# A time-mixing and MoE kernel on one core: unit 0 in two halves, three weight tiles in plain fp32, ten tiles of block 1 in halves, a new order table

## The chip, the cores and the metric

The kernel runs on one core of a Trainium2 chip. It uses TensorE (PE in the profile, with its weight loads as PEld), VectorE (DVE), ScalarE (ACT), GpSimd (POOL), SyncE (SP, which issues nearly all loads and stores), and the 16 DMA engines. The metric is the device time of one execution, in microseconds (us). Before the change it was 486.84 us, the median of three.

## The reference

Two stages, all in fp32. The first is a recurrence over 768 positions for 4 batches and 8 heads of 48 channels; the second is a two-layer network over the 3072 tokens that it gives.

```python
for t in range(S):                                    # S = 768
    cur = np.einsum('bhd,bhe->bhde', u[None] * kt, vt)
    y[:, :, t] = np.einsum('bhd,bhde->bhe', rt, state + cur)
    state = wt[:, :, :, None] * state + np.einsum('bhd,bhe->bhde', kt, vt)
...
h = x @ w_in                                          # (3072, 384) @ (384, 2048)
g = np.where(h >= 1, h, np.where(h <= -1, 0, (h + 1) ** 2 / 4))
out = g @ w_out                                       # (3072, 2048) @ (2048, 384)
```

## The kernel before, in words

**First stage.** The 768 positions are cut into 12 units of 64 positions (256 tokens over the four batches). `attention(u)` does one unit. Its heads come in two groups q = 1 and q = 0. For each group DVE scans the decays w from the end (`scan`, L451) and from the start (L456) and scales k and r by them (`scaled`, L474); ACT forms u times k (`with_u`, L479). PE multiplies r with u times k (the diagonal) and scaled r with scaled k, in 32 products of 64 x 64 each (`among`, L508). DVE picks the diagonal of the first result and the upper part of the second into R by masked copies (`picked`, L516). PE transposes k (L558), forms the state (`umat`, L583), and multiplies R and the old state with v and r (`along` and `crossed`, L618). Units 0 and 1 have one head per group spread over three places; PE brings it there (`spread`, L709). ACT then writes x rounded to fp32r (x high, L688), PE subtracts it in PSUM (`less`, L699), and ACT writes the rest (x low, L684).

**Second stage.** Six blocks of 512 tokens, two units each; 16 weight tiles of 128 columns of the hidden layer (ff tiles). A product of fp32 accuracy is made of three fp32r products (high x high, high x low, low x high), so nine matmuls of one tile into the hidden layer (`product_in`, L1262) and nine out of it (`product_out`, L1282). Between them ACT and DVE apply the gate (L1062, L1063, L1072) and split g into high (ACT, L1074) and low (DVE, L1075). Weight tiles are loaded as raw bits, put together into the fp32 tile `fl` by two ACT passes and two DVE passes (L347, L352, L366, L369), and split into high (L343 on ACT, for two tiles L341 on DVE) and low (L373). There are three `fl` buffers. Where a unit's x is there before the block's second unit, tiles are done for 256 tokens at a time ("in halves"): block 0 for tiles 0 to 4, block 1 for tiles 0 to 13. Blocks 3 to 5 use a scheme with fewer products (L932).

**Order.** Every step is entered into a list by `op`; the table `ORDER` gives the order in which the steps are emitted to the engines' queues, `BANKS` which of the eight PSUM banks each result gets, and `FILLS` where products of zeros (`zeros`, L298) are put in on PE. Each engine works through its queue in that order and waits where its operands or its bank aren't ready. So the names ps, rk, xf, x, fl in the profile are tiles; rk holds r and k, wq the decays, cst the constants.

Of the kernel before, what the change touches and what calls it, by code (L numbers as in the profile page):

```python
# [25 lines left out]
C = 64  # L26
# [10 lines left out]
PAIRED = [(i, i + 1) for i in range(0, 14, 2)]  # L37
# [95 lines left out]
)  # L133
FILLS = (
    (42, 0, 256, False), (50, 0, 512, False), (54, 0, 384, False),
)

LOW = 7.499 * 2.0**-32


class Plan:
# [26 lines left out]
    def emits(self, fill):  # L168

        put_in = {n: x for n, *x in FILLS}  # L170
        for n in ORDER:
            if n in put_in:
                fill(*put_in[n])
            self.ops[n]["emit"]()
# [1171 lines left out]
```

## Time and profile before

| | us |
|---|---|
| three timed executions | 486.79, 486.84, 489.51 |
| median | 486.84 |
| the profiled execution, first to last instruction | 489.6 |
| PE, DVE, ACT, POOL busy in it | 470.8, 403.1, 301.8, 28.1 |

No other time is given for the profiled execution than its span. PE busy is the time in which at least one matmul is in the array; matmuls overlap, so the time from one row's start to the next row's start tells more than the sum of durations. A timeline row merges instructions of one form; its second number reaches from the first start to the last end. The clock column gives the granted clock as a share of 2.4 GHz.

### The profile page before, as it was taken

Reading aid. Unit: us, or ns where it says so; the run is one execution under the profiler, and the core shown is the slowest. Engines: PE = TensorE matmul, PEld = TensorE weight load, DVE = VectorE, ACT = ScalarE, POOL = GpSimd, SP = SyncE. Lnnn points to the kernel's source line nnn. Section 1 sums busy time; section 2 is a strip of 40 time slices with the busy share of each in tenths; the row PEclk is TensorE's granted clock in tenths of the full one; section 3 lists DMA queues with packets and bytes.
Section 4 is the critical chain, followed back from the end, with each engine's and each line's share of the span. In section 5 each row is a group of like instructions: output and inputs, shape, how many; then the busy total and the mean of one; then the engine's idle time right before and its main releaser. Section 6 shows DMA issues by size and latency. Waiting matters only on the chain.

```text
span 489.6 us, 13368 instructions
## 1 busy us (share of the span) xinstructions
PE 470.8 (96%) x5709; PEld 417.4 (85%) x5709; DVE 403.1 (82%) x627; ACT 301.8 (62%) x582; POOL 28.1 (6%) x49
## 2 busy tenths in 40 slices
PE   2899999999999999999999999999999999999994
PEld 2689888889999999888888888999889999889984
DVE  6899999999897888798998977889687657585682
ACT  4788988854635276365655567855846656776560
POOL 4000000000000000000000033412300000000000
PEclk9999999999999999999999999999999999999998
DMA  8939646324650435243444201110010111121102
GB/s 317 384 134 325 263 174 205 105 70 147 199 169 3 148 111 170 100 168 105 149 154 138 85 3 50 46 23 15 9 39 28 45 23 21 33 76 44 23 1 72
DMA packets 35205, 53.53 MB, mean 109 GB/s; under 512 B 15744, under 2 KB 22592, under 8 KB 35136
## 3 DMA queue, kind: packets, MB, share of 16 engines
q1 hardware_dynamic: 34992, 52.45, 32.3%
q8 instruction: 47, 0.77, 0.7%
q14 instruction: 22, 0.18, 0.1%
q10 hardware_dynamic: 144, 0.13, 0.1%
HBM read 46.86 MB, written 4.72 MB: 105 GB/s over the span
## 4 chain that ended last, share of the span: by engine, by line
PE 85%; DVE 5%; DMA 5%; issue 2%; SPq 2%; ACT 1%; DVEq 0%
PE ps L1262 37%; PE ps L932 19%; PE ps L1282 18%; PE ps L618 4%; PE ps L508 3%; PE ps L558 2%; DMA rk<-in_rk 2%; DMA wq<-in_w 2%; PE ps L583 2%; DMA nk<-in_nk 1%; DVE y L451 1%; SPq L730 1%; SPq L280 1%; DVE fl L369 1%; DVE rk L474 0%
## 5 line engine op out<-in xcount | busy, mean ns | idle before, releaser
L1262 PE MATMUL ps<-x,wt 128*128 128x512 f32 (+1 forms) x1035 | 214.0, 357 | 0.1
L1262 PEld LDWEIGHTS ps<-x,wt 128*128 128x128 f32 x1035 | 168.1, 188 | 26.8 <-DVE rk L894 0.4
L1282 PE MATMUL ps<-gh,wt 128*128 128x256 f32 (+1 forms) x402 | 79.3, 332 | 0.4 <-DVE g L1072 0.4
L1282 PEld LDWEIGHTS ps<-gh,wt 128*128 128x128 f32 x402 | 61.5, 188 | 7.9 <-DVE g L1072 0.6
L892 ACT ACTIVATE rk<-ps 128x512 f32<-128x512 f32 x48 | 28.4, 597 | 46.3 <-PE ps L1262 27.3
L894 DVE SCALAR_TENSOR_TENSOR rk<-rk,ps 128x512 f32<-128x512 f32 x48 | 32.6, 684 | 24.1 <-ACT rk L893 23.9
L1062 ACT ACTIVATE g<-ps 128x512 f32<-128x512 f32 (+1 forms) x49 | 28.7, 588 | 34.7 <-PE ps L1262 23.1
L1282 PE MATMUL ps<-gl,wt 128*128 128x256 f32 (+1 forms) x201 | 44.1, 328 | 0.0
L1074 ACT CAST gh<-g 128x512 fp32r<-128x512 f32 (+1 forms) x49 | 29.5, 609 | 18.4 <-DVE g L1072 18.4
L1072 DVE SCALAR_TENSOR_TENSOR g<-g,ps 128x512 f32<-128x512 f32 (+1 forms) x49 | 32.2, 665 | 6.3 <-ACT g L1063 6.3
L1075 DVE TENSOR_TENSOR gl<-g,gh 128x512 fp32r<-128x512 f32 (+1 forms) x49 | 32.9, 678 | 4.1 <-ACT gh L1074 3.9
L1282 PEld LDWEIGHTS ps<-gl,wt 128*128 128x128 f32 x201 | 32.3, 188 | 3.6
L451 DVE TENSOR_TENSOR_SCAN y<-wq,ends 128x520 f32<-128x520 f32 x24 | 29.6, 1234 | 5.5 <-POOL r L289 3.8
L900 DVE TENSOR_TENSOR g_again<-rk,nk_again 128x512 fp32r<-128x512 f32 x35 | 24.5, 711 | 11.3 <-ACT nk_again L899 11.2
L900 DVE TENSOR_TENSOR gl<-rk,gh 128x512 fp32r<-128x512 f32 x36 | 25.1, 704 | 9.6 <-ACT gh L899 9.5
L1063 ACT ACTIVATE g<-g 128x512 f32<-128x512 f32 (+1 forms) x49 | 30.0, 622 | 0.4
L893 ACT ACTIVATE rk<-rk 128x512 f32<-128x512 f32 x48 | 29.4, 630 | 0.5
L456 DVE TENSOR_TENSOR_SCAN p<-wq,seeds 128x520 f32<-128x520 f32 x24 | 29.7, 1237 | 0.0
L899 ACT CAST gh<-rk 128x512 fp32r<-128x512 f32 x36 | 22.1, 617 | 7.7 <-DVE rk L918 3.9
L899 ACT CAST nk_again<-rk 128x512 fp32r<-128x512 f32 x35 | 21.5, 617 | 5.7 <-DVE rk L894 3.5
L932 PE MATMUL ps<-nk_again,wt 128*128 128x256 f32 x130 | 24.9, 281 | 0.0
L851 POOL TENSOR_TENSOR p<-wt 128x256 f32<-128x256 f32 x8 | 6.9, 873 | 294.0 <-DVE p L851 294.0
(165 smaller groups left out, 842.5 us busy)
## 6 DMA issues: line engine op xcount, KB each, us to landing
rk<-in_rk SPq DMA_DIRECT2D x18, 512.0 KB, 4.1
wraw<-in_wbits SPq DMA_DIRECT2D x11, 768.0 KB, 6.2
nk<-in_nk SPq DMA_DIRECT2D x9, 768.0 KB, 4.6
wq<-in_w SPq DMA_DIRECT2D x24, 261.5 KB, 3.5
wraw<-in_wbits SPq DMA_DIRECT2D x15, 256.0 KB, 5.9
vn<-in_v SPq DMA_DIRECT2D x9, 384.0 KB, 4.6
rk<-in_rk SPq DMA_DIRECT2D x12, 256.0 KB, 5.8
last<-in_w SPq DMA_DIRECT2D x12, 256.0 KB, 3.0
```

The costliest lines, as they stand in the source:

```text
L451: V.tensor_tensor_scan(out=y_[:, ::-1], data0=w[:, SEG:0:-1], data1=ends.rearrange("p n c -> p (n c)")[:, ::-1], initial=0.0, op0=ALU.mult ...
L456: V.tensor_tensor_scan(out=pv[:, q].rearrange("p n c -> p (n c)"), data0=w[:, 0:SEG], data1=sv, initial=0.0, op0=ALU.mult, op1=ALU.add)
L894: op("DVE", 0.68, [("b", ht)], [qk], lambda: V.scalar_tensor_tensor(out=gf, in0=gf, scalar=1.0, in1=at(ht), op0=ALU.min, op1=ALU.max))
L899: op("ACT", 0.6, [key], fresh_in(("h", i, k)), lambda: A.copy(spare(k, i), x))
L900: op("DVE", 0.67, [key, ("h", i, k)], fresh_in(("l", i, k)), lambda: V.tensor_tensor(out=spare(k, 3 + i), in0=x, in1=spare(k, i).bitcast(F ...
L932: PE.matmul(at(sums_at[b][i])[:, half * UT : half * UT + UT], lhsT=w[wi], rhs=g[gi], start=(b, i) not in opened, stop=True, skip_group_che ...
L1063: op("ACT", c, (), [("g", gk)], lambda: A.activation(gs, gs, AF.Square))
L1072: op("DVE", 0.15 + 0.53 * k, [("b", ht)], [("g", gk)], lambda: V.scalar_tensor_tensor(out=gs, in0=gs, scalar=1.0, in1=hs(), op0=ALU.min, o ...
L1074: op("ACT", c, [("g", gk)], [("gh", gk)], lambda: A.copy(ghs, gs))
L1075: op("DVE", 0.145 + 0.54 * k, [("g", gk), ("gh", gk)], [("gl", gk)], lambda: V.tensor_tensor(out=gls, in0=gs, in1=ghs.bitcast(F32), op=ALU ...
L1262: nc.tensor.matmul(hp, lhsT=wx[f][:, cs], rhs=xt[:, j, :], start=first and n == 0, stop=n == 8, skip_group_check=not first)
L1282: nc.tensor.matmul(o[j], lhsT=wx[f][:, cs], rhs=gt, start=first and i == 0, stop=stop and i == 2, skip_group_check=True)
```

## The change

- Unit 0's diagonal and upper products, the masked copies and the products with v are done for the heads of q = 1 and q = 0 apart (`PARTED`, `picked_of`).
- Unit 0's x is also written as plain fp32 (`x32`). In block 0, the first 256 tokens meet weight tiles 0, 1 and 2 in plain fp32 (`product_in_f32`, `product_out_f32`): three matmuls in and three out instead of nine and nine, from `fl` before it is split, and g isn't split. The three tiles' split forms are still made for the other tokens.
- Block 1 does ten tiles in halves, where it did fourteen.
- `FILLS` has eight zero products (2,496 columns in all) where it had three (1,152), and one step can be given several.
- `ORDER` and `BANKS` are new throughout. The loads of the constants and of unit 0's v come earlier in SP's queue.

```diff
-PAIRED = [(i, i + 1) for i in range(0, 14, 2)]
+PAIRED = [(i, i + 1) for i in range(0, 10, 2)]
 HALVES = {0: (((0,), (1, 2), (3, 4)), ((0, 1), (2, 3), (4,))), 1: (PAIRED, PAIRED)}
...
 ORDER = (
-    1, 0, 14, 6, 9, 5, 7, 15, 3, 16, 2, 56, 19, 4, 22, 17, 8, 18, 27, 97, 104, 111, 28, 26, 30, 31, 29, 21, 33, 40, 35, 32, 23, 43, 34,
...
+    1, 14, 15, 2, 18, 0, 16, 4, 8, 11, 17, 7, 52, 19, 3, 27, 21, 22, 103, 115, 5, 10, 28, 62, 30, 20, 23, 64, 12, 29, 26, 31, 24,
...
 FILLS = (
-    (42, 0, 256, False), (50, 0, 512, False), (54, 0, 384, False),
+    (46, 6, 512, False), (46, 6, 64, False), (40, 5, 512, False), (45, 2, 512, False), (45, 2, 64, False), (57, 7, 256, False),
+    (86, 7, 512, False), (86, 7, 64, False),
 )
...
+PARTED = {0}
+PLAIN = {0, 1, 2}
...
+    x32 = flat(xf[1], 512, 1280).rearrange("p (a t) -> p a t", t=UT)
...
+        def picked_of(of, mask, q):
+            V.copy_predicated(
+                out=r_[:, :, 2 * q : 2 * q + 2].rearrange("p h a b c -> p h (a b) c"),
+                mask=mask.unsqueeze(1).unsqueeze(1).broadcast_to([128, 2, 4, C]),
+                data=two(of)[:, :, 256 * q : 256 * q + 256].rearrange("p h (n c) -> p h n c", c=C))
...
+        if early and parted:
+            bd = plan.tenant(2)
+            for q in (1, 0):
+                op("PE", 0.48, [("ku", q), "nk", ("r", slot[q])], [("bq", bd, q)], lambda q=q: among(
+                    bd, lambda q: ku[:, q], lambda q: raw(q, 0), mine(q)), code=64, small=True, touch=[bd])
+                op("DVE", 0.7, [("bq", bd, q), "cst"], R_of(q), lambda q=q: picked_of(bd, twice.bitcast(I32), q), touch=[bd])
+        elif early:
...
+        if parted and u == 0:
+            op("PE", 0.48, [*R_of(1), vk, ("vpad", 0), rs[1]], [("b", by)], lambda: along((2,)), fresh=False, code=64, small=True)
+            op("PE", 0.48, [*R_of(0), vk, ("vpad", 0), rs[0]], [("bq", by, 0)], lambda: along((0,)), fresh=False, code=64, small=True, touch=[by])
...
+        if u == 0:
+            op("ACT", 0.8, [("b", by), ("bq", by, 0)], ["x32"], lambda: A.copy(
+                x32.rearrange("p a (c g t) -> p a c g t", c=2, g=2), two(by).rearrange("p g (a c t) -> p a c g t", a=4, t=C)[:, 0:3]))
...
+        plain = b == 0 and cs == halves[0] and set(fs) <= PLAIN
+        for i, f in enumerate(fs if plain else ()):
+            op("PE", 1.4, [("fl", f % FULL), "x32", *after], [("b", ht)], lambda i=i, f=f: product_in_f32(
+                nc, at(ht)[:, i * w : i * w + w], fl[f % FULL], x32, not i), fresh=not i, code=12)
...
+            if not plain:
+                op("ACT", c, [("g", gk)], [("gh", gk)], lambda: A.copy(ghs, gs))
+                op("DVE", 0.145 + 0.54 * k, [("g", gk), ("gh", gk)], [("gl", gk)], lambda: V.tensor_tensor(
+                    out=gls, in0=gs, in1=ghs.bitcast(F32), op=ALU.subtract), port=True)
...
+            if plain:
+                op("PE", 1.4, [("g", gk), ("fl", f % FULL)], [("b", acc[j]) for j in range(3)], fresh=begin, code=12,
+                   emit=lambda f=f, mine=mine, begin=begin: product_out_f32(
+                       nc, [at(t)[:, cs] for t in acc], fl[f % FULL], gs[:, mine], begin))
+                continue
...
+def product_in_f32(nc, hp, s, x, first=True):
+    for n, j in enumerate((2, 0, 1)):
+        nc.tensor.matmul(hp, lhsT=s[:, j * 128 : j * 128 + 128], rhs=x[:, j, :], start=first and n == 0, stop=n == 2, skip_group_check=not first)
...
+def product_out_f32(nc, o, s, g, first):
+    for j in range(3):
+        cs = slice(384 + j * 128, 384 + j * 128 + 128)
+        nc.tensor.matmul(o[j], lhsT=s[:, cs], rhs=g, start=first, stop=False, skip_group_check=True)
```

PE at the start of the program. The names are result tile <- operands (ps is PSUM, zero the tile of zeros, cst the constants, xf scaled r or k of unit 0, rk_83 and rk_82 raw r, nk u times k). Before:

```order
L558 MATMUL ps_110<-cst_67,xf_109 128x128 x4
L305 MATMUL ps_110<-zero_75 64x128 x2
L508 MATMUL ps_110<-rk_83,nk_85 64x64 x16
L508 MATMUL ps_110<-rk_82,nk_85 64x64 x16
L651 LDWEIGHTS zero_75
L651 MATMUL ps_110<-zero_75 128x512
...
L298 MATMUL ps_110<-zero_75 128x256
L508 MATMUL ps_110<-xf_108 64x64 x16
L508 MATMUL ps_110<-xf_108,xf_109 64x64 x16
```

Now:

```order
L314 MATMUL ps_110<-zero_75 64x128 x2
L690 LDWEIGHTS zero_75
L690 MATMUL ps_110<-zero_75 128x512
...
L307 MATMUL ps_110<-zero_75 128x512
L307 MATMUL ps_110<-zero_75 128x64
L588 MATMUL ps_110<-cst_67,xf_109 128x128 x4
L307 MATMUL ps_110<-zero_75 128x512
L518 MATMUL ps_110<-rk_83,nk_85 64x64 x16
L518 MATMUL ps_110<-xf_108,xf_109 64x64 x16
L518 MATMUL ps_110<-rk_82,nk_85 64x64 x16
```

The first transposes move behind the warm-up, the clearing of the banks of unit 0's output and one zero product of 576 columns; a second zero product of 512 stands behind them, and the 32 products of each kind become two times 16, the two kinds in turn.

DVE at the end of unit 0's work (r is R; below and cst give the masks; xf is scaled k or r; y the scan from the end; wraw and fl are weight steps). Before:

```order
L456 SCALAR_TENSOR_TENSOR p_87<-wq_80,seeds_73 128x520
L451 SCALAR_TENSOR_TENSOR y_88<-wq_81,ends_74 128x520
L474 TENSOR_TENSOR xf_108<-rk_83,p_87 128x512
L516 COPY_PREDICATED r_90<-cst_67,ps_110 128x1024
L366 TENSOR_SCALAR wraw_133<-fl_107 128x768
L516 COPY_PREDICATED r_90<-below_71,ps_110 128x1024
L486 RECIPROCAL seeds_73<-y_88 128x8
```

Now:

```order
L466 SCALAR_TENSOR_TENSOR p_87<-wq_80,seeds_73 128x520
L531 COPY_PREDICATED r_90<-cst_67,ps_110 128x2x256
L484 TENSOR_TENSOR xf_108<-rk_83,p_87 128x512
L531 COPY_PREDICATED r_90<-below_71,ps_110 128x2x256
L531 COPY_PREDICATED r_90<-cst_67,ps_110 128x2x256
L375 TENSOR_SCALAR wraw_134<-fl_107 128x768
L531 COPY_PREDICATED r_90<-below_71,ps_110 128x2x256
L461 SCALAR_TENSOR_TENSOR y_88<-wq_81,ends_74 128x520
```

Two masked copies of 1024 columns have become four of 2 x 256, the second half's copies behind the first half's, and unit 1's first scan (L451, now L461) moves from ahead of them to behind them.

PE at the end of unit 1's work and the first products of the network (x_94 is block 0's x, xf_109 holds x32, fl the fp32 weights, wt the split weights, g the gate's output). Before:

```order
L618 MATMUL ps_110<-rk_82,st_93 48x64 x8
L618 MATMUL ps_110<-rk_84,st_93 48x64 x8
L1262 MATMUL ps_110<-x_94,wt_366 128x256 x9
L618 MATMUL ps_110<-rk_82,st_93 48x64 x8
L618 MATMUL ps_110<-rk_84,st_93 48x64 x8
L618 MATMUL ps_110<-r_90,vn_86 48x64 x32
L583 MATMUL ps_110<-vn_86,kt_91 64x48 x32
L709 MATMUL ps_110<-ob_106,nk_85 128x128 x6
L1262 MATMUL ps_110<-x_94,wt_600 128x256 x9
L699 MATMUL ps_110<-x_94,minus_69 128x128 x6
L1262 MATMUL ps_110<-x_94,wt_615 128x256 x9
L1262 MATMUL ps_110<-x_94,wt_366 128x256 x9
```

Now:

```order
L657 MATMUL ps_110<-rk_84,st_93 48x64 x8
L588 MATMUL ps_110<-cst_67,rk_82 128x128 x4
L1224 MATMUL ps_110<-g_97,fl_107 128x256 x3
L1224 MATMUL ps_110<-g_98,fl_107 128x256 x3
L657 MATMUL ps_110<-rk_82,st_93 48x64 x8
L657 MATMUL ps_110<-rk_84,st_93 48x64 x8
L657 MATMUL ps_110<-r_90,vn_86 48x64 x32
L622 MATMUL ps_110<-vn_86,kt_91 64x48 x32
L753 MATMUL ps_110<-ob_106,nk_85 128x128 x6
L1224 MATMUL ps_110<-g_98,fl_107 128x256 x3
L743 MATMUL ps_110<-x_94,minus_69 128x128 x6
L1334 MATMUL ps_110<-x_94,wt_616 128x256 x9
```

The nine-matmul products between unit 1's steps become groups of three; when unit 1's correction (x_94, minus) is emitted, three tiles are through both layers for the first 256 tokens (six half products), where four had been through the first layer alone.

## Rows read from the trace of the kernel before

**Rows 1.** The page, busy us, share and instructions of each engine.

```profile
PE 470.8 (96%) x5709; PEld 417.4 (85%) x5709; DVE 403.1 (82%) x627; ACT 301.8 (62%) x582; POOL 28.1 (6%) x49
```

**Rows 2.** Waits of PE: engine, line, releaser; us in total, times, longest.

```profile
PE ps L558 <- DVE xf L474: 8.7, 1, 8.7
PE ps L508 <- ACT nk L479: 0.6, 1, 0.6
```

**Rows 3.** Windows: stretch, us, busy PE, PEld, DVE, ACT, POOL (instructions), clock, DMA, GB/s.

```profile
0.00:5.00 5.00, 0.00 (x0) 0.00 (x0) 1.23 (x1) 1.28 (x1) 2.92 (x15) 1.00 0.58 197
5.00:10.00 5.00, 1.28 (x6) 0.98 (x8) 4.97 (x9) 2.27 (x7) 1.28 (x3) 1.00 1.02 386
```

**Rows 4.** Timeline of POOL: start, us, line, operation [idle before, releaser].

```profile
8.72 0.70 POOL L443 COPY nk<-cst 128x32 f32<-128x32 f32 x1 [5.03 <-DMA cst<-in_consts]
```

**Rows 5.** Timeline of PE, 8 to 20 us.

```profile
8.72 1.09 PE L558 MATMUL ps<-cst,xf 128*128 128x128 f32 x4 [8.72 <-DVE xf L474]
...
10.48 1.99 PE L508 MATMUL ps<-rk,nk 64*64 64x64 f32 x64
...
14.14 0.69 PE L508 MATMUL ps<-xf 64*64 64x64 f32 x32
...
18.45 1.58 PE L709 MATMUL ps<-ob,nk 128*128 128x128 f32 x12
```

**Rows 6.** Timeline of ACT, 5 to 21 us.

```profile
5.08 0.91 ACT L479 ACTIVATE nk<-rk,wq 128x256 f32<-128x256 f32 x2 [2.82 <-DMA rk<-in_rk]
...
11.34 0.29 ACT L427 ACTIVATE minus<-cst 128x128 fp32r<-128x128 f32 x1
...
20.19 0.79 ACT L688 CAST x<-ps 128x768 fp32r<-128x768 f32 x1
```

**Rows 7.** Timeline of DVE, 10 to 33 us.

```profile
10.43 1.21 DVE L451 TENSOR_TENSOR_SCAN y<-wq,ends 128x520 f32<-128x520 f32 x1
...
12.70 1.31 DVE L516 COPY_PREDICATED r<-cst,ps 128x1024 f32<-128x1024 int32 x1 [0.47 <-ACT wraw L352]
...
15.37 1.30 DVE L516 COPY_PREDICATED r<-below,ps 128x1024 f32<-128x1024 int32 x1 [0.86 <-PE ps L508]
...
22.80 0.56 DVE L341 CAST wt<-fl 128x768 fp32r<-128x768 f32 x1
...
30.35 0.95 DVE L373 TENSOR_TENSOR wt<-fl,wt 128x768 fp32r<-128x768 f32 x1
...
31.21 1.33 DVE L516 COPY_PREDICATED r<-below,ps 128x1024 f32<-128x1024 int32 x1
```

**Rows 8.** Timeline of PE, 32 to 70 us.

```profile
32.38 0.67 PE L618 MATMUL ps<-rk,st 64*48 64x64 f32 x32
...
36.15 1.42 PE L1262 MATMUL ps<-x,wt 128*128 128x256 f32 x9
...
37.48 0.89 PE L699 MATMUL ps<-x,minus 128*128 128x128 f32 x6
...
38.20 3.39 PE L1262 MATMUL ps<-x,wt 128*128 128x256 f32 x27
...
52.07 2.23 PE L1262 MATMUL ps<-x,wt 128*128 128x512 f32 x9
...
54.14 0.87 PE L1282 MATMUL ps<-gh,wt 128*128 128x256 f32 x6
...
55.20 2.23 PE L1262 MATMUL ps<-x,wt 128*128 128x512 f32 x9
...
68.62 1.16 PE L508 MATMUL ps<-rk 64*64 64x64 f32 x64
```

**Rows 9.** The page, costliest groups: count, busy us, mean ns, idle before.

```profile
L1075 DVE TENSOR_TENSOR gl<-g,gh 128x512 fp32r<-128x512 f32 (+1 forms) x49 | 32.9, 678 | 4.1 <-ACT gh L1074 3.9
```

**Rows 10.** Timeline of ACT, 104 to 140 us: unit 3's x.

```profile
107.17 0.80 ACT L682 COPY xf<-ps 128x768 f32<-128x768 f32 x1 [0.93 <-PE ps L618]
```

**Rows 11.** Timeline of DVE, 104 to 140 us: unit 3's x.

```profile
137.66 0.96 DVE L1040 TENSOR_TENSOR x<-xf,x 128x768 fp32r<-128x768 f32 x1
```

More of the change, by code (lines that the diff above doesn't have):

```diff
@@ L145, in __init__, with add @@
         self.tenants, self.where = [], BANKS
-    def add(self, engine, cost, emit, reads=(), writes=(), port=0, size=0, fresh=True, code=0, small=False):
+    def add(self, engine, cost, emit, reads=(), writes=(), port=0, size=0, fresh=True, code=0, small=False, touch=()):
         n = len(self.ops)
+        for t in touch:
+            self.tenants[t]["users"].append(n)
         deps = {self.writer[x] for x in (*reads, *writes) if x in self.writer}
@@ L288, in attention_moe @@
         for h in range(2):
-            op("POOL", 0.5, (), [("R", h)], lambda h=h: G.memset(r_[:, h], 0.0))
+            op("POOL", 0.5, (), [("R", h, q) for q in range(2)], lambda h=h: G.memset(r_[:, h], 0.0))
     last_f = ob[:, 0:UT]
@@ L496, in attention, with among @@
         dv = d_.rearrange("p c (a h) -> p h a c", h=2)
-        def among(to, left, right):
-            for pair in range(4):
+        def among(to, left, right, pairs=range(4)):
+            for pair in pairs:
                 q, pr = divmod(pair, 2)
@@ L511, in among @@
                             )
-        both_R = [("R", 0), ("R", 1)]
+        both_R = [("R", h, q) for q in range(2) for h in range(2)]
         def picked(of, mask):
@@ L518, in picked, with R_of, mine @@
                 data=two(of).rearrange("p h (n c) -> p (h n) c", c=C))
-        if early:
+        def picked_of(of, mask, q):
[3 more added lines that the diff above has]
+                data=two(of)[:, :, 256 * q : 256 * q + 256].rearrange("p h (n c) -> p h n c", c=C))
+        def R_of(q):
+            return [("R", h, q) for h in range(2)]
+        def mine(q):
+            return range(2 * q, 2 * q + 2)
+        parted = u in PARTED
+        if early and parted:
[5 more added lines that the diff above has]
+        elif early:
             bd = plan.tenant(2)
@@ L545, in attention @@
             for h in range(2):
-                op("DVE", 0.68, ["d", "cst"], [("R", h)], lambda h=h: V.tensor_tensor(
+                op("DVE", 0.68, ["d", "cst"], [("R", h, q) for q in range(2)], lambda h=h: V.tensor_tensor(
                     out=r_[:, h], in0=twice.unsqueeze(1).unsqueeze(1).broadcast_to([128, 4, 2, C]),
@@ L558, in ktrans @@
                     PE.transpose(out=at(b)[:, lo : lo + 128], in_=ready(q, 1)[:, tokens(pr, c2)], identity=ident)
-        op("PE", 0.95, [*ks, *rs], [("b", ba)],
-           lambda: among(ba, lambda q: ready(q, 1), lambda q: ready(q, 0)), code=128, small=True)
+        if parted:
+            for q in (1, 0):
+                op("PE", 0.48, [ks[q], rs[q]], [("bq", ba, q)], lambda q=q: among(
+                    ba, lambda q: ready(q, 1), lambda q: ready(q, 0), mine(q)), code=64, small=True, touch=[ba])
+        else:
+            op("PE", 0.95, [*ks, *rs], [("b", ba)],
+               lambda: among(ba, lambda q: ready(q, 1), lambda q: ready(q, 0)), code=128, small=True)
         goes_on = u < NU - 1
@@ L568, in attention @@
                     kt[:, 2 * q : 2 * q + 2].rearrange("p a b c -> p (a b c)"), at(b)))
-        op("DVE", 1.32, [("b", ba), "below"], both_R, lambda: picked(ba, below))
+        if parted:
+            for q in (1, 0):
+                op("DVE", 0.7, [("bq", ba, q), "below"], R_of(q), lambda q=q: picked_of(ba, below, q), touch=[ba])
+        else:
+            op("DVE", 1.32, [("b", ba), "below"], both_R, lambda: picked(ba, below))
         bu = plan.tenant(2) if goes_on else None
@@ L819, in attention_moe @@
     st_keys = [[("spad", i), ("s", i)] for i in range(2)]
-    R_keys = [("R", 0), ("R", 1)]
+    R_keys = [("R", h, q) for q in range(2) for h in range(2)]
     olds = [(("w", 0),), (("w", 1),), (("w", 2),), ("y",), ("seeds",), *[fl_keys] * 4, R_keys, R_keys, *[vn_keys] * 3, *st_keys]
@@ L1098, in attention_moe @@
     attention(1)
+    early_steps = [n for n, (b, fs, cs) in enumerate(steps) if b == 0 and cs == halves[0] and set(fs) <= PLAIN]
     for f in range(NF):
         weight(f)
+        for n in early_steps:
+            if steps[n][1][-1] == f:
+                products(n)
     for n, (b, fs, cs) in enumerate(steps):
@@ L1117, in attention_moe @@
                 divided(b + 1)
-        if n < len(steps) - 1:
+        if n < len(steps) - 1 and n not in early_steps:
             products(n)
```

25 lines of the change are left out of this document (13 added, 12 removed), and 158 rows, old and new, of tables (BANKS, ORDER).

## The prediction, made before the changed kernel was timed

> **What bounds the kernel now.** I read the page's busy line first: TensorE (PE) is busy for 470.8 of 489.6 us, VectorE (DVE) for 403 [rows 1]. So little is left to win on PE except where it stands still. The list of waits says where that is [rows 2]: one wait of 8.7 us ahead of its first product, and then pieces of 0.6 us and less. The change is therefore judged in the first 70 us: how early PE gets steady work, and how much work that is.
>
> The wait of 8.7 us is put down to a DVE multiplication, but the same constants that PE's transposes need are what GpSimd's copy waits for, and they come at 8.72 [rows 4, 5]. They are the seventh load. DMA moves 197 GB/s in the first 5 us and 386 GB/s after [rows 3]. From there unit 0 goes back and forth: 32 small products from 10.48, DVE's masked copy (12.70), which the next 32 wait for since they share a PSUM bank (14.14), and the second masked copy, done at 16.67 [rows 5, 7]. In this stretch PE is slow: 64 records take 1.99 us at 10.48 and 1.16 us for the same shape at 68.62 [rows 5, 8]. The granted-clock column reads 1.00 (the 2.4 GHz level) in both early stretches [rows 3], so it is the durations that show this.
>
> **Removed and added products.** Weights 0 to 2 met unit 0 in 54 products of 256 columns. Nine of those take 1.06 us (54.14 to 55.20) [rows 8], so 6.4 us go. In come 18 plain fp32 products of 256 columns, a form the trace lacks. Six fp32 products of 128 columns take 1.58 us [rows 5], which is at most 0.26 each and 0.53 for 256 columns; less the tail that overlaps the next instruction it is about 0.45. From below, each has two records where the old form has one, so at least 2 x 0.118 = 0.24. I take 0.45, the nearer row: 8.1 us, or 1.7 more PE work than before.
>
> Ten instead of fourteen weight tiles of block 1 go in halves: 72 products of 512 columns replace 144 of 256, eight groups of nine. A group of nine takes 2.07 us at 512 columns (52.07 to 54.14) against twice 1.06 [rows 8], so 8 x 0.05 = 0.4 us go, on a PE that has no other work to wait for there. The Trainium skill, "TensorE: Matmul & The Clock Gate", section "Back-to-back issue gap", gives N/2.4 + 2.5 ns between warm products; by that rule the 72 pairs would save 72 x 2.5 ns = 0.2 us, an estimate. This case's spacing (118 and 230 ns) is longer at both widths, and the measurement decides.
>
> On DVE two subtractions go, 256 and 512 columns wide, at most 0.68 us each [rows 9], and their two ScalarE (ACT) casts. One ACT copy of x of 0.8 us comes in [rows 6], the time of the copy of the same shape. Two masked copies of 1.3 us become four of half the size; a half costs between 0.65 (proportional) and 1.3; I take 0.70, near the proportional end; each 0.1 more would put 0.3 us on the path of unit 0.
>
> **What is moved in the queues.** The constants become the third load: 96 KB behind the first 773 KB, which have landed at 5.08 [rows 6]. At 386 GB/s they land near 5.3. Unit 0's v (384 KB) now goes ahead of the weights, and unit 1's scan input and half of its k and r ahead of the third weight, which so comes 0.9 MB, or 2.3 us, later. It lands near 16 and DVE takes it up near 22, so this stays hidden behind unit 1's scans; that cover gone, it would delay the third plain product one to one.
>
> **Unit 0, step by step.** PE's first zero product of 576 columns shares a bank with the warm-up products, which ACT has to read first, behind its copy of the constants (0.29) [rows 6]: it starts at 5.8. At 0.235 per 128 fp32 columns it is 1.06 us, and 2.1 at the early slow rate: 7.9. Transposes, 1.0 as now: 8.9. The second zero product stands in the way again: 0.94 or 1.9, I take 1.4: 10.3. Sixteen small products (0.5 to 1.0, taken 0.6): 10.9. DVE had come free at 10.43 [rows 7] and waits until 11.05. Then masked copy (0.70), scaling (0.6), second masked copy, first copy of the other half, one weight step (0.5): 14.4. PE meanwhile has the other half's 16 products, transposes, and a third zero product of 576 columns (1.06), and ends the last 16 at 14.9. The last masked copy ends at 15.7, where it ended at 16.67 before. But the first scan of unit 1, 1.21 us, was done by then and now comes after.
>
> DVE has no idle time from there. Before, it took 15.87 us from 16.67 to the end of unit 1's second masked copy (31.21 + 1.33) [rows 7]. Now three low-part subtractions (3 x 0.95) and a cast (0.56) come later and the scan (1.21) is added: 13.7. That gives 29.4. One half-wide gate instruction, 0.4 us: 29.8.
>
> From there PE works through unit 1's remaining products, which took 5.82 us from 32.38 to 38.20 less the 1.33 of the nine products at 36.15 [rows 8], so 4.5, and nine plain output products, 4.05. It ends unit 1's correction at 38.35, against 38.20 before. At that point it has done six half products of the network, where the old order had done four. The two are worth 2.1 us. Up to the masked products of unit 2 at 68.62 the old order took 30.4 us; the new one has 2.1 less, so it is **2.0 us ahead** there. I keep the old 0.6 us wait [rows 2] in that: in the new order a similar one falls where PE wants the fourth and fifth weight before DVE has split them.
>
> **Sum.** 2.0 + 0.4 = 2.4 us off the profiled span, 489.6 to 487.2. That span lies 2.8 us above the median of the three times, 486.84, and near the highest. I take the difference over to the median: **484.4 us**, no more than 0.5%. About 1%, 4.9 us, is what a measurement of this kernel can tell from no change. The unknowns set this case's own range: with plain products at 0.24, nine of them on the path, 1.9 less; with the slow rate through the sixteen and the second zero product, 0.9 more, and plain products at 0.53, 0.7 more. So 482.5 to 486.0. Chance 0.55.
>
> **Rivals.** *The front is quicker.* If PE runs at its full rate from 5.8, the zero products no longer stand in the way, DVE does its first masked copy at 10.43 without waiting, and the last ends near 14.4: 1.3 us more. If DVE also keeps the weights ahead of PE, the 0.6 us goes too: 482.5. For it: PE's first products now wait only for the zeros that GpSimd writes within its first 2.92 us of work [rows 3], not for a load. Against it: they leave a gap of about two us before 5.8, and the old kernel was still slow 1.7 us after its first product [rows 5]. The Trainium skill, same page, section "What's actually happening", says that the array starts throttled and activity releases it, and that the point varies from run to run. By that rule this rival holds when release falls early in the zero products; the old trace agrees that PE starts slow and then is not. Chance 0.18.
>
> *The lead is given back.* DVE itself gains little: once it has done the postponed 3.4 us as well it stands at 32.8, where it stood at 32.5 before [rows 7]. If DVE and not PE sets the pace until unit 3 is through, only the two dropped subtractions (1.1) count and the new order must make up the rest; one more wait of a microsecond, as the eight zero products or new bank neighbours can make, and nothing is left: 486.5. Against it: PE shows hardly any wait in this stretch now [rows 2]. Chance 0.17.
>
> *Slower: the second half of block 1 comes late.* With ten tiles in halves, PE has four half products in and four out fewer to do before it must have unit 3's x. In the new order some 17.5 us of PE work lie between unit 3's last product and the first one that needs that x. Before, its copy began at 107.17 and its low part was ready at 138.6 [rows 10, 11], over 31 us later. That was the order's choice, since nothing needed it. The shortest chain (two copies, six small loads, cast, subtraction) is some 9 us. It decides once the chain takes more than 17.5 us; as long as before, PE would stand for 14 us, and half-way, at 24.5 us, for 7: 484.4 + 7 = 491.4. Against it: the loads stand early in the queue. Chance 0.05. Five more in a hundred go to other losses of a new order over 400 us that I can't place, 488 and above.
>
> **Range and chances.** From 481.8 to 488.0 the first three cases lie nearly whole. Left out are the far end of the quick front below (0.09) and the last two cases above (0.10), 2 in 10 at most. Faster by over 1% (below 482.0) only if a quick front meets cheap plain products: 0.10. Slower by over 1% (above 491.7): 0.04. Within 1%: 0.86.
>
> **What would show it.** PE's first product before 3 us and its first transposes near 8, not 8.7 to 9; half-size masked copies near 0.7; the last of unit 0 at 15.7; plain products 0.45 apart; unit 1's correction ending near 38.3; unit 2's masked products near 66.3; from there on a steady lead of 2 us that grows by 0.4 in block 1. Wrong would be: a PE wait of over 1 us at the fourth or fifth weight, or before block 1's second half; a lead at 66 us that is gone at 120; a quick front shown by the masked copies ending before 15.

## The result, and the profile after

The changed kernel takes **494.1 us** (median of four, 491.56 to 494.41) where the kernel before, beside it, takes 487.06. The ratio is **1.0115, with a 95% interval from 1.0085 to 1.0145**: slower by about 1%, or 5.6 us. (The two medians alone lie 7.0 us apart. Of four times each, one of the changed kernel is 2.4 us below the next and one of the kernel before 2.2 us above the next, so the text goes by the ratio and its interval.) The forecast was 484.4 us, in a range from 481.8 to 488.0.

The page of the profiled execution (493.96 us, span 492.4), the line that answers to [rows 1]:

```profile
PE 476.5 (97%) x5629; PEld 414.9 (84%) x5629; DVE 405.9 (82%) x627; ACT 308.4 (63%) x581; POOL 27.9 (6%) x49
```

PE's waits after the change (line, releaser; us in total, times, longest), answering to [rows 2]:

```profile
PE ps L314 <- POOL zero L292: 2.2, 1, 2.2
PE ps L307 <- ACT look L318: 1.9, 1, 1.9
PE ps L1334 <- DVE rk L941: 1.6, 2, 1.1
PE ps L307 <- DVE r L531: 1.5, 1, 1.5
PE ps L979 <- ACT gh L946: 0.8, 1, 0.8
```

The wait of 8.7 us is gone, as forecast; PE's first wait is now for the zeros (L314), 2.2 us. Two waits of zero products (L307) have come, and two at the line of the network's products into the hidden layer (L1334) and in the fast blocks (L979), which have no counterpart in [rows 2]. The windows say where those are. Columns as in [rows 3], after the change:

```profile
280.00:300.00 20.00, 19.56 (x181) 15.95 (x180) 12.03 (x22) 12.04 (x23) 6.25 (x9) 1.00 0.15 33
300.00:320.00 20.00, 18.98 (x123) 16.85 (x122) 15.80 (x28) 17.01 (x34) 5.65 (x7) 1.00 0.32 79
320.00:345.00 25.00, 23.49 (x145) 20.54 (x144) 17.39 (x32) 19.83 (x42) 6.91 (x9) 1.00 0.28 64
```

PE is busy for 62.0 of these 65 us; in both traces of the kernel before (the second is below) it is busy throughout. So PE stands for 3.0 us here, far behind the 70 us that the prediction looked at. In the same 65 us ACT stands for a tile named `last`:

```profile
ACT last L794 <- DMA last<-in_w: 10.4, 10, 3.4
```

What that is: for each of units 0 to 5 and each head group the kernel loads the decays once more, into one buffer (`last`), and ACT checks with two instructions (an absolute value, L794, and a sum of what is over 1, L795) that none is over 1. These twelve **guards** have nothing to do with the edit; the new order table has only put them elsewhere. The rows of that tile between 285 and 345 us after the change:

```profile
L289 SPq DMA_DIRECT2D last<-in_w x11: 367/368/393, 291.9 to 341.1; - x11
L794 ACT ACTIVATE last<-last x11: 627/632/634, 295.3 to 344.0; 128x512 f32<-128x512 f32 x11
...
DMA to landing us min/median/max: 1.8/3.0/3.7
```

Eleven loads within 49.2 us, one every 4.9 us. A load takes 3.0 us from issue to landing, the two instructions and the read of the sum 0.63 + 0.72 + 0.19 us, and only then can the next load start: 4.5 us. The chain is all but tight, and its steps aren't evenly placed: at ten of the eleven guards ACT stands, for 0.15 to 3.41 us. ACT takes its queue in order, so what stands behind L794 waits too. The first time, on ACT, DVE and PE:

```profile
291.24 0.62 ACT L946 CAST gh<-rk 128x512 fp32r<-128x512 f32 x1
295.27 0.63 ACT L794 ACTIVATE last<-last 128x512 f32<-128x512 f32 x1 [3.41 <-DMA last<-in_w]
...
297.78 0.63 ACT L940 ACTIVATE rk<-rk 128x512 f32<-128x512 f32 x1
```

```profile
298.45 0.69 DVE L941 SCALAR_TENSOR_TENSOR rk<-rk,ps 128x512 f32<-128x512 f32 x1 [3.69 <-ACT rk L940]
```

```profile
299.19 2.33 PE L1334 MATMUL ps<-x,wt 128*128 128x512 f32 x9 [0.44 <-DVE rk L941]
302.33 0.50 PE L979 MATMUL ps<-gh,wt 128*128 128x256 f32 x2 [0.80 <-ACT gh L946]
```

ACT has stood for 3.41 us, so the gate's second ACT step (L940) comes late; DVE's gate (L941) waits 3.69 us for it, and PE has no work left and stands.

### The profile page after: what moved, and what is told of

It is laid out like the page before. It is cut to its first block, busy times and chain, and to the rows that moved or that the text cites. A ratio compares the mean times of both kernels' runs of the same rounds, so it can differ in the third digit from the quotient of the medians.

```text
span 492.4 us, 13209 instructions
## 1 busy us (share of the span) xinstructions
PE 476.5 (97%) x5629; PEld 414.9 (84%) x5629; DVE 405.9 (82%) x627; ACT 308.4 (63%) x581; POOL 27.9 (6%) x49
## 4 chain that ended last, share of the span: by engine, by line
PE 83%; DMA 8%; ACT 4%; issue 2%; DVE 1%; SPq 1%; ACTq 0%
PE ps L1334 35%; PE ps L1354 19%; PE ps L979 15%; DMA last<-in_w 6%; PE ps L657 4%; PE ps L518 3%; PE ps L588 2%; PE ps L622 2%; PE ps L307 1%; ACT last L795 1%; ACT last L794 1%; PE ps L1218 1%; DMA wraw<-in_wbits 1%; DMA cst<-in_consts 1%; SPq L777 1%
## 5 line engine op out<-in xcount | busy, mean ns | idle before, releaser
L1334 PE MATMUL ps<-x,wt 128*128 128x512 f32 (+1 forms) x972 | 208.0, 366 | 2.0 <-DVE rk L941 1.6
L1334 PEld LDWEIGHTS ps<-x,wt 128*128 128x128 f32 x972 | 162.9, 188 | 30.2 <-DVE rk L941 2.4
L1354 PE MATMUL ps<-gh,wt 128*128 128x512 f32 (+1 forms) x360 | 75.3, 344 | 0.0
L941 DVE SCALAR_TENSOR_TENSOR rk<-rk,ps 128x512 f32<-128x512 f32 x48 | 32.9, 685 | 39.0 <-ACT rk L940 38.4
L1354 PEld LDWEIGHTS ps<-gh,wt 128*128 128x128 f32 x360 | 57.4, 188 | 7.7
L1354 PE MATMUL ps<-gl,wt 128*128 128x512 f32 (+1 forms) x180 | 42.0, 342 | 0.0
L1354 PEld LDWEIGHTS ps<-gl,wt 128*128 128x128 f32 x180 | 30.0, 188 | 4.2
L461 DVE TENSOR_TENSOR_SCAN y<-wq,ends 128x520 f32<-128x520 f32 x24 | 29.6, 1233 | 3.9 <-POOL st L301 3.7
L940 ACT ACTIVATE rk<-rk 128x512 f32<-128x512 f32 x48 | 30.2, 631 | 1.0
L979 PE MATMUL ps<-nk_again,wt 128*128 128x256 f32 x130 | 24.8, 281 | 0.0
```

The costliest lines, as they stand in the source:

```text
L461: V.tensor_tensor_scan(out=y_[:, ::-1], data0=w[:, SEG:0:-1], data1=ends.rearrange("p n c -> p (n c)")[:, ::-1], initial=0.0, op0=ALU.mult ...
L940: op("ACT", c, (), [qk], lambda: A.activation(gf, gf, AF.Square))
L941: op("DVE", 0.68, [("b", ht)], [qk], lambda: V.scalar_tensor_tensor(out=gf, in0=gf, scalar=1.0, in1=at(ht), op0=ALU.min, op1=ALU.max))
L979: PE.matmul(at(sums_at[b][i])[:, half * UT : half * UT + UT], lhsT=w[wi], rhs=g[gi], start=(b, i) not in opened, stop=True, skip_group_che ...
L1334: nc.tensor.matmul(hp, lhsT=wx[f][:, cs], rhs=xt[:, j, :], start=first and n == 0, stop=n == 8, skip_group_check=not first)
L1354: nc.tensor.matmul(o[j], lhsT=wx[f][:, cs], rhs=gt, start=first and i == 0, stop=stop and i == 2, skip_group_check=True)
```

## The experiments

All ratios are to the kernel before, run beside the kernel in question on the same chip, with 95% intervals. They are the record's figures over all runs and not the quotients of the two medians. Rows were run on several chips, so kernels are compared by their ratios.

| kernel | median us (runs) | before beside it | ratio |
|---|---|---|---|
| a_spread: guards at their old places | 491.31 (10) | 488.33 | 1.0064 [1.0034, 1.0094] |
| b_bunched: before, guards packed | 495.02 (4) | 488.33 | 1.0132 [1.0079, 1.0186] |
| a_nofill: no zero products | 497.16 (4) | 488.33 | 1.0162 [1.0103, 1.0221] |
| a_banks: zero products in other banks | 491.75 (11) | 488.31 | 1.0068 [1.0040, 1.0095] |
| a_best1: a_spread and a_banks | 489.05 (12) | 488.31 | 1.0003 [0.9980, 1.0025] |
| a_noguard: no guards | 489.40 (11) | 488.31 | 0.9999 [0.9973, 1.0025] |
| b_const: before, constants loaded third | 488.09 (12) | 488.31 | 0.9982 [0.9954, 1.0009] |
| a_best2: guards in ACT's gaps, a_banks | 485.99 (12) | 487.69 | 0.9962 [0.9940, 0.9985] |
| a_best3: a_best2, five zero products | 487.03 (12) | 487.69 | 0.9966 [0.9937, 0.9995] |
| a_spread_nofill: a_spread, no zero products | 491.60 (11) | 487.69 | 1.0060 [1.0034, 1.0087] |
| a_noload: guards packed, one load | 489.00 (12) | 488.12 | 1.0010 [0.9983, 1.0037] |

**A second trace of before** (b_again, no edit).

> The kernel before, unchanged, for a second trace of it. Its first trace has a span of 489.6 us, which with the 1.55 us around a span makes 491.1, while its median is 487.06. Theory 'untypical trace': the new span is 485 to 486 us, and the 4 us of difference lie in one stretch of few microseconds (the start, where the first trace's first matmul came at 8.72 us, is the likeliest). Rival 'profiling costs 4 us': the new span is again 489 to 490, and the difference between trace and timed runs is spread or lies in the recording itself.

The span was 486.9 us, between the two expectations. By the spacing of PE's products, the first trace falls 1.6 us behind this one by 60 us (0.9 of it near 48 us) and 1.3 more between 130 and 150 us. It was an execution at the slow end, and the second is the one to compare with. In it the guards' loads are spread from 306 to 451 us, and no row says that anyone waited for one:

```profile
L280 SPq DMA_DIRECT2D last<-in_w x12: 367/390/1407, 306.1 to 451.5; - x12
L747 ACT ACTIVATE last<-last x12: 615/628/636, 309.4 to 458.4; 128x512 f32<-128x512 f32 x12
```

At points where PE has done the same products in both traces, the changed kernel is 0.9 us behind this trace at 99 us, 0.8 behind at 277, 6.3 at 383 and 5.7 at the end. So 5.5 us are lost between 277 and 383 us: 3.0 of them PE stands, and in the rest its products follow each other more slowly while it counts as busy.

**Guards spread** (a_spread). In the table 1130 + 3i is guard i's load, the next two its ACT steps, 1733 the check of their results.

```diff
 ORDER = (
-    ... 1088, 1218, 1130, 1198, 1089, ... 1092, 1219, 1131, 1167, 1132, 1093, ...
+    ... 1088, 1218, 1198, 1089, ... 1092, 1219, 1167, 1093, ...
+    ... 1100, 1215, 1130, 1230, 1227, ... 1239, 1228, 1131, 1101, 1232, ... 1108, 1237, 1132, 1247, ...
```

> The changed kernel with one thing moved: the twelve guard loads into the one buffer 'last' with their two ScalarE operations each, which the changed order packs into 290 to 350 us, stand at the places that they have beside TensorE's work in the kernel before (spread over 300 to 455 us); the check that reads their maxima moves behind the last. Theory 'guards': ScalarE no longer stands for 'last' (10.4 us in that stretch before the move), the gates of block 2 and of the first fast block come in time, TensorE's idle time between 280 and 345 us goes from 3.0 us to under 0.7, and the time falls by 4 to 5 us to 489 to 490. Rival 'the order itself': the gates are late through their own new places, the guards only fill the hole; the time stays at 493 to 495.

The ratio fell from 1.0115 to 1.0064; PE stands for none of the 65 us (the last 25 of them are shown), and ACT for `last` 2.5 us in all from 280 to 460 us:

```profile
ACT last L795 <- DMA last<-in_w: 2.5, 4, 1.3
```

```profile
320.00:345.00 25.00, 25.00 (x162) 22.66 (x161) 19.15 (x40) 17.36 (x35) 8.22 (x9) 1.00 0.05 11
```

The rival is out: the gates are not late at their own new places. But 0.5% is half of the loss, less than expected. By the spacing of its products the kernel with spread guards still loses 2.3 us more than one without guards between 280 and 470 us, in small pieces; with better places (a_best2, below) these are not lost.

**Guards packed in the kernel before** (b_bunched): the reverse move.

```diff
 ORDER = (
-    ... 1211, 1099, 1136, 1213, 1235, ... 1220, 1101, 1137, 1102, 1103, ... 1270, 1109, 1138, 1271, ...
+    ... 1210, 1251, 1136, 1098, 1211, 1137, 1138, 1099, 1213, ... 1232, 1241, 1139, 1104, 1140, 1141, 1237, ...
```

> The kernel before with the reverse move: its twelve guard loads and their ScalarE operations packed beside the same TensorE work as in the changed kernel (some 300 to 360 us, 10 us later than there because the buffer must be free). Nothing else changes. Theory 'guards': ScalarE stands for 'last', TensorE waits 2 to 4 us between 300 and 365 us, and the time rises from 487 to 490 or 491. Rival 'the order itself': the packing alone is harmless, 487 within 0.7.

From 1 to 1.0132, more than expected. ACT's row for `last` (290 to 372 us) and PE's new waits, in the kernel before:

```profile
ACT last L750 <- DMA last<-in_w: 10.2, 8, 4.2
```

```profile
PE ps L935 <- DVE kt_again L913: 2.1, 1, 2.1
PE ps L1265 <- DVE rk L897: 1.2, 1, 1.2
PE ps L935 <- ACT kt_again L912: 1.1, 1, 1.1
```

**No guards, and guards without loads** (a_noguard, a_noload).

```diff
-                    load(w.rearrange(...), a["w"][u, q]..., ["guard", *fresh_in("guard")])
-                    guard(w, "guard", i)
+                    op("SP", 0.45, (), ["guard", *fresh_in("guard")], lambda: None)
+                    op("ACT", 0.63, (), ["guard"], lambda: None)
+                    op("ACT", 0.2, ["minus_one"], ["guard", ("above", i)], lambda i=i: A.copy(above[:, i : i + 1], minus_one))
```

```diff
+                    if i == 0:
                         load(w.rearrange(...), a["w"][u, q]..., ["guard", *fresh_in("guard")])
+                    else:
+                        op("SP", 0.45, (), ["guard"], lambda: None)
                     guard(w, "guard", i)
```

> The changed kernel without the twelve guard loads and their 24 ScalarE operations (it leaves out the check of units 0 to 5 against the bound; a copy of one column a guard fills the table that the check reads). Theory 'guards': all that the packed guards cost comes back, and 0.5 to 1.5 us more than with them spread, since ScalarE has 16 us less to do: 489.5 to 491. Rival 'the order itself': what the guards held up is late without them too; over 492.5.

> The changed kernel with eleven of the twelve guard loads left out; all 24 ScalarE operations stay in their packed places and work on the data of the first load (so the check of units 0 to 5 sees one slice only). Theory 'the wait for the load': ScalarE's 10.4 us of standing for 'last' are gone, and nearly all of the 5.6 us come back, ratio to the kernel before 0.999 to 1.003, as without guards (0.9999). Rival 'ScalarE's own work': 16 us of operations packed between the gates are what makes the gates late; ratio 1.007 to 1.0115, as the changed kernel (1.0115).

0.9999 and 1.0010: both give the whole 1.1% back, a_noguard more than expected. a_noload is the one that decides between the wait and the work. It has all 24 ACT instructions in the packed places; ACT is busier there than in the changed kernel (20.57 us of 25 from 320 to 345 us, against 19.83), and yet PE stands for 0.3 us of the 65 only. Of ACT's 10.4 us of standing 3.1 are left, for the one load:

```profile
ACT last L794 <- DMA last<-in_w: 3.1, 1, 3.1
```

```profile
280.00:300.00 20.00, 19.90 (x182) 16.24 (x181) 12.39 (x22) 12.89 (x24) 6.59 (x10) 1.00 0.10 20
300.00:320.00 20.00, 19.78 (x128) 17.77 (x127) 16.30 (x31) 18.07 (x38) 6.72 (x7) 1.00 0.11 40
320.00:345.00 25.00, 25.00 (x161) 22.70 (x160) 20.29 (x39) 20.57 (x43) 6.63 (x9) 1.00 0.00 1
```

So it is the wait for the load at the head of an in-order queue that costs; what ACT's own time adds is too small to tell (1.0010 against 0.9999, with intervals of 0.3% either way). With the loads their DMA traffic goes too, but in the same 65 us of the changed kernel no wait of PE, DVE, ACT or POOL ends on a DMA except ACT's for `last`. The Trainium skill, "Trainium Kernel Development and Optimization", section "Best Practices", asks for two buffers so that DMA overlaps compute; the trace agrees, with one buffer and 10.4 us of standing. (A second buffer was not tried.) The Trainium skill, "DMA: Bandwidth & Descriptors", section "Anatomy of one DMA — SWDGE (gpsimd) path", gives 2.0 us plus bytes over 436 GB/s for loads that GpSimd issues, which makes 2.6 us for these 256 KB, an estimate; the 3.0 measured here, for loads that SP issues, decides.

**Zero products in other banks** (a_banks).

```diff
 FILLS = (
-    (46, 6, 512, False), (46, 6, 64, False), (40, 5, 512, False), (45, 2, 512, False), (45, 2, 64, False), (57, 7, 256, False),
+    (46, 7, 512, False), (46, 7, 64, False), (40, 5, 512, False), (45, 5, 512, False), (45, 5, 64, False), (57, 7, 256, False),
```

> The changed kernel with two of its zero products (of 576 columns each) written to other PSUM banks: the first to one that the warm-up products do not use, the third to one that VectorE's masked copy is not reading. In the changed kernel's trace the first waits 1.9 us for ScalarE's look at the warm-up bank and the third 1.5 us for that masked copy, and PE's transposes and the last 16 small products of unit 0 stand behind them. Theory 'the zero products' banks hold unit 0 up': the first transposes begin at 5.5 to 6.5 us and not at 7.92, the last masked copy of unit 0 ends 1.0 to 1.5 us before 16.57, and the time falls by 1.0 to 1.5 us (492.5 to 493 on the scale of 494.1). Rival 'VectorE sets the pace in the front': it is busy with scans up to 10.5 us and from 16 us on, PE waits elsewhere, and the time is the same within 0.5.

1.0068 against 1.0115: 0.5%, or 2.3 us, more than expected, though the two intervals overlap a little. Unit 0 on PE, first in the changed kernel, then in a_banks:

```profile
5.74 2.39 PE L307 MATMUL ps<-zero 128*128 128x512 f32 x4 [1.91 <-ACT look L318]
7.92 1.06 PE L588 MATMUL ps<-cst,xf 128*128 128x128 f32 x4
...
11.19 0.65 PE L518 MATMUL ps<-rk,nk 64*64 64x64 f32 x32
...
13.96 1.29 PE L307 MATMUL ps<-zero 128*128 128x512 f32 x4 [1.53 <-DVE r L531]
15.18 0.69 PE L518 MATMUL ps<-xf 64*64 64x64 f32 x32
```

```profile
3.62 2.23 PE L307 MATMUL ps<-zero 128*128 128x512 f32 x4
5.95 0.97 PE L588 MATMUL ps<-cst,xf 128*128 128x128 f32 x4
...
11.51 1.19 PE L307 MATMUL ps<-zero 128*128 128x512 f32 x4
13.20 0.69 PE L518 MATMUL ps<-xf 64*64 64x64 f32 x32 [0.50 <-DVE r L531]
```

And DVE's last masked copy of unit 0, in the changed kernel and in a_banks:

```profile
15.94 0.73 DVE L531 COPY_PREDICATED r<-below,ps 128x512 f32<-128x512 int32 x1 [0.95 <-PE ps L518]
```

```profile
14.24 0.72 DVE L531 COPY_PREDICATED r<-below,ps 128x512 f32<-128x512 int32 x1
```

A zero product of 576 columns that nobody needs had stood in front of the last 16 small products, waiting for a bank that DVE was reading. In a free bank it runs in PE's pause. The first zero product, which had waited 1.91 us for ACT, comes 2.1 us sooner. With both, unit 0 is done 1.7 us sooner.

The edit does one thing more. The trace keeps a list of the changes of PE's granted clock. Its first entry is a rise to the full 2.4 GHz, at 9.74 us in the changed kernel and at 6.63 us in a_banks; before it there is no entry, and there the clock column reads 1.00 whatever the clock was. In the four traces with the old banks (after, a_spread, a_noguard, a_noload) the rise lies between 9.74 and 12.18 us, and near 98 us they are 0.8 to 2.0 us behind the second trace of before. In the four with the other banks (a_banks, a_best1, a_best2, a_best3) it lies between 5.57 and 6.80 us, and they are 0.8 to 1.3 us ahead. So the gain of the front is clear. How much of it is the wait for the banks and how much the earlier rise was not separated.

**Without zero products** (a_nofill, a_spread_nofill).

```diff
-FILLS = (
-    (46, 6, 512, False), (46, 6, 64, False), (40, 5, 512, False), ...
-)
+FILLS = ()
```

> The changed kernel without its eight zero products (an empty table; nothing else moves). They read no data and nobody reads them, and take 6 to 7 us of TensorE between 5.7 and 20.2 us and at the places behind it. Theory 'front': those at 16.25 and 19.01 us (0.66 and 1.13 us to the next instruction) lie on TensorE's path, the others in waits; 0.5 to 1.8 us faster, 492.3 to 493.6. Rival 'they buy the clock': the granted clock falls to half in some stretch of the first 25 us, and the time is the same or up to 3 us more.

> The changed kernel with the guards spread and without any zero product. With the guards packed, leaving the zero products out made it 3 us slower, of which the trace showed 1.1 us by 45 us and 4.4 us in the stretch of the guards. Theory 'the rest was the guards': with the guards spread the loss is 0.5 to 1.5 us against 491.3 (492 to 493). Rival 'the zero products are worth 3 us in every case': 494 to 495. Rival 'they only cost': under 491.

With the guards packed the ratio without them is higher (1.0162 against 1.0115), though the intervals overlap; with the guards spread no difference can be told (1.0060 against 1.0064, each within 0.3% either way). So with the old banks the zero products neither bring nor cost more than some 2 us in all; a loss of 0.5 to 1.5 us without them, as expected, is not excluded. What they do is visible. The twelve records of the products that bring the spread head to its places (L753, in a_nofill L750), in the changed kernel and without zero products:

```profile
16.91 1.58 PE L753 MATMUL ps<-ob,nk 128*128 128x128 f32 x12
```

```profile
16.24 2.90 PE L750 MATMUL ps<-ob,nk 128*128 128x128 f32 x12 [0.58 <-ACT ob L754]
```

Without them PE pauses for 2.2, 1.6 and 1.1 us and works at nearly half its rate up to 20 us. The clock list agrees: its first entry, the rise, comes at 20.77 us in a_nofill and at 20.41 in a_spread_nofill, against 9.74 in the changed kernel. So the rival of a_nofill was right on the clock: the zero products buy an earlier rise, and take about as much time as that saves.

In a_nofill's trace, which is of the slowest of its four executions (499.2 us), the packed guards held PE up longer than in the changed kernel, and after that its clock fell:

```profile
320.00:345.00 25.00, 20.98 (x124) 17.94 (x123) 15.73 (x29) 17.87 (x36) 7.14 (x9) 1.00 0.24 54
345.00:365.00 20.00, 20.00 (x125) 18.29 (x126) 15.32 (x28) 12.64 (x26) 0.46 (x1) 0.91 0.14 34
```

Why the same guards stood longer there than in the changed kernel was not tested.

**Constants alone** (b_const): in the kernel before, the one load moved.

```diff
 ORDER = (
-    1, 0, 14, 6, 9, 5, 7, 15, 3, 16, 2, 56, 19, 4, 22, 17, 8, 18, 27, ...
+    1, 0, 14, 6, 9, 5, 7, 15, 18, 3, 16, 2, 56, 19, 4, 22, 17, 8, 27, ...
```

> The kernel before with one part of the change alone: the load of the constants (96 KB) is the third on its queue, where it was the seventh. PE's first transposes waited for it until 8.71 us. Theory 'VectorE sets the pace in the front': the transposes begin at 5.5 to 6 us, but the first masked copy starts at 12.2 to 12.7 as before since VectorE is busy with its scans, 0 to 0.5 us faster. Rival 'the constants': 1 us faster or more, since the products behind the transposes come earlier.

No difference that can be told (0.9982, with 1 inside the interval). PE's first products come 2.7 us sooner and then wait:

```profile
6.02 1.11 PE L561 MATMUL ps<-cst,xf 128*128 128x128 f32 x4 [6.02 <-DVE xf L477]
...
10.48 1.99 PE L511 MATMUL ps<-rk,nk 64*64 64x64 f32 x64 [2.72 <-ACT look L312]
```

The first masked copy starts at 12.70 us, as in [rows 7]. These 2.7 us of the old profile's longest wait were off the path. (The clock's rise came later with it, at 15.93 us against 13.60 in the second trace of before.)

**Both causes taken away** (a_best1, a_best2, a_best3). a_best1 has the edits of a_spread and a_banks. a_best2 puts each ACT step of a guard where ACT stands idle in the trace of a_noguard, and the load behind the step before it:

```diff
 ORDER = (
+    ... 1048, 1049, 1131, 1132, 1133, 1200, 1094, ... 1192, 1209, 1134, 1210, 1213, ... 1101, 1232, 1135, 1136, 1233, ...
```

a_best3 drops the last three zero products from that.

> Both edits in the changed kernel: the guard loads at the places of the kernel before, and the two zero products in other banks. If the two causes are independent: 491.3 less 1.0 to 1.5, so 489.8 to 490.3 where the kernel before is 488.3, ratio 1.003 to 1.004. If VectorE sets the pace of the front, 491.3 again, ratio 1.006.

> The changed kernel with its zero products in the other banks, and the twelve guards placed one by one: each Abs and each Relu at a place where ScalarE stands idle for 0.9 us or more in the trace without guards (between 296 and 427 us), each load right behind the Relu before it. Theory 'two independent causes': the 5.6 us of the guards and the 2.3 us of the banks both come back, TensorE's excess behind 255 us falls from 4.7 (spread) to under 3, and the time is 485.5 to 487 on the scale where the kernel before is 488.3: ratio 0.995 to 0.998. Rival 'a guard costs wherever it stands' (12 x 1.35 us of ScalarE in a stretch where gates wait for it): as with the guards spread, ratio 1.000 or above.

> As the one before, and without the last three zero products (256, 512 and 64 columns; 16.3 and 19.0 us in the changed kernel's trace, 0.66 and 1.13 us to the next instruction). Theory 'VectorE sets the pace there': nothing in the time, within 0.5 us of the one before. Rival 'they lie on TensorE's path': 1 to 1.8 us faster. Rival 'they keep TensorE quick': the products behind them take longer and it is 0.5 to 1.5 us slower.

1.0003 (1.003 to 1.004 was expected), then **0.9962 [0.9940, 0.9985]**: 0.4% faster than the kernel before, and 1.5% faster than the changed one. The two causes add up: the steps from 1.0115 to a_banks and to a_noguard are 0.5% and 1.2%, together 1.6%, and 1.0115 less 0.9962 is 1.5%. a_best3 (0.9966) differs from a_best2 by less than can be told; its median is 1.0 us higher, so that the three zero products bring something is not excluded. That they cost 1 us or more is unlikely. In a_best2 PE is busy throughout from 280 to 370 us:

```profile
320.00:345.00 25.00, 25.00 (x163) 22.75 (x162) 18.06 (x34) 18.06 (x36) 8.81 (x9) 1.00 0.10 22
```

## Why the prediction was wrong

**The step that failed** is its first: "The change is therefore judged in the first 70 us". No term stood for what the new order does behind that; "other losses of a new order over 400 us that I can't place" got 5 in 100. They could have been placed. Both orders list the guards' loads and ACT steps with the products between them, and the durations are in a trace of before: 3.0 us a load, 1.5 us of ACT, one buffer, so a guard can't follow another in less than 4.5 us without ACT standing. The new order has them 4.9 us apart on average, with nothing to spare where two fall closer, the old one 13. Of the 5.6 us lost, all are given back without the guards or without their loads. The forecast was a ratio of 0.995 (484.4 to 486.84); the guards' 1.2% and the 0.5% of the zero products' banks are about the distance from there to 1.0115, and without both causes (a_best2) the ratio is 0.9962.

**The front**, forecast at 2.0 us ahead: at 64 us it is 0.8 ahead of the first trace and 0.8 behind the second. By the steps:

- Right: PE's first product before 3 us (2.17); the first zero product held by ACT's look and begun at 5.8 (5.74); transposes at 7.9 (7.92); half masked copies near 0.7 (0.73); the second half of block 1 without a wait.
- Right in size: plain fp32 products at 0.45. Their five rows, each up to the next row's start, make 8.1 us for the 18 products, as in the sum, though one row gives 0.37 each and another 0.54. Two of them: 12 records (6 products) from 31.12 to 33.91, 0.46 each, and 6 records from 22.50 to 23.94, 0.48 each.

```profile
22.50 1.51 PE L1218 MATMUL ps<-xf,fl 128*128 128x256 f32 x6
23.94 1.16 PE L518 MATMUL ps<-rk,nk 64*64 64x64 f32 x64
...
31.12 2.86 PE L1224 MATMUL ps<-g,fl 128*128 128x256 f32 x12 [0.27 <-DVE g L1123]
33.91 0.67 PE L657 MATMUL ps<-rk,st 64*48 64x64 f32 x32
```

- Wrong: DVE's first masked copy was to start at 11.05, behind 16 small products. It started at 11.96, 0.12 us after the last of three groups of 16 (11.19 + 0.65). It does so in a_banks too (10.44 + 0.65, then 11.21), and the halves share banks in the kernel, so the first half still waited for the second half's products. The profile itself names no releaser for this wait (`issue`).

```profile
11.96 0.73 DVE L531 COPY_PREDICATED r<-cst,ps 128x512 f32<-128x512 int32 x1 [1.48 <-issue]
```

- Wrong: "a third zero product of 576 columns (1.06)" was costed by its duration alone. It also waits 1.53 us for the masked copy that reads its bank. The last masked copy ended at 16.67, not 15.7, and [rows 7] have 16.67 too. a_banks, which frees the first zero product as well, gives 2.3 us, about what the forecast had as its whole gain.
- Read wrongly: the clock column's 1.00 in the first 10 us as the 2.4 GHz level. It stands for a time without an entry; the clock rose at 14.00 us in the trace that the prediction read, so the slow durations that it went by were right. It put the first zero product at the slow rate and the second between the two rates (1.4 us); the rise came at 9.74 us, within the second (1.43 us, from 8.78 to 10.21).
- From there the error is carried on: unit 1's correction ends 1.4 us later than forecast (39.73, not 38.35), unit 2's masked products begin at 67.51, not 66.3 (the prediction's own sum gives 66.6).

```profile
38.96 0.94 PE L743 MATMUL ps<-x,minus 128*128 128x128 f32 x6
39.73 1.52 PE L1334 MATMUL ps<-x,wt 128*128 128x256 f32 x11
...
67.51 1.16 PE L518 MATMUL ps<-rk 64*64 64x64 f32 x64
```

The same products in the second trace of before:

```profile
67.05 1.16 PE L508 MATMUL ps<-rk 64*64 64x64 f32 x64
```

**The carry-over to the median.** The prediction took a difference within one trace and put it on a median 2.8 us lower. The second trace shows that 1.6 us of the first one's first 60 us were that execution's own, so part of the expected lead was over a time that the usual execution doesn't take.

**The halves of block 1** were to save 0.4 us. At points where both have done the same products, the distance to the second trace is 0.9 us at 99 us, 0.35 at 216 and 0.96 at 256. So half a microsecond is won up to 216 us and lost again by 256, and nothing of it is left in the total; what gave it and what took it is open.

**The rivals.** "The lead is given back" had the front right: nothing is left of the lead against the second trace, and a wait of a zero product on a bank, which this rival names, is part of it. It did not have the 5.6 us. "The front is quicker" did not occur; in a_banks, with the rise at 6.63 us, the last masked copy of unit 0 ends at 14.96, nearer to the 14.4 of this rival. "The second half of block 1 comes late" did not occur. The slower side came by a mechanism that was not among them.

## What to carry to other kernels

When an order table changes, look not only at what was edited: for every single buffer that a chain of loads goes through, divide the stretch in which the new order places the chain by its length, and compare with load plus use; an in-order engine that meets such a load too early holds up all that stands behind it. A product put in only to keep PE busy must go to a bank that nobody reads at that time, or it becomes a wait itself. And a wait that heads the list may be off the path: what it releases has to be followed to the engine that is busy at that time.

## What the runs showed of the hardware that was not expected

- After pauses of 1.1 to 2.2 us in the first 16 us PE took 2.90 us for what it did in 1.58 us with zero products in those pauses, with 1.00 in the clock column both times. The Trainium skill, "TensorE: Matmul & The Clock Gate", section "What's actually happening", says that the clock is throttled by default and that activity releases it; the durations and the trace's clock list agree with that, with the rise at 20.77 us without zero products and at 9.74 us with them. The column doesn't show it, since the list has no entry before the rise.
- In the middle of a run the clock fell once: in a_nofill PE had been busy for 20.98 of 25 us and had just stood for 2.63 us when the list shows half the clock, 1.2 GHz, from 345.03 us for 3.41 us. The nine products of 512 columns begun there took 3.76 us, where nine before them (337.37 to 339.43) took 2.06.
- Executions of one kernel differ by more than a per cent: 486.56 to 492.62 us in 35 runs of the kernel before on one chip. A single trace is one draw from that.
